# Stage 1's attention shares divided ahead of their transposes, two block sums of V on GpSimd, and a new order

## The chip, the cores and the metric

One core of a Trainium2 chip runs the whole program. The metric is the device time of one execution in microseconds, as the median of the runs; lower is better. TensorE (PE) multiplies, VectorE (DVE), ScalarE (ACT) and GpSimd (POOL) work on tiles, and SyncE (SP) issues nearly all transfers. Each engine takes its instructions strictly in the order in which they stand in its own queue.

## The reference

Attention with a window and with block summaries, and a feed-forward network on its result. Four batches of eight heads, 768 tokens, heads of 64; the model has 512 columns, the network 2048.

```python
k_sum = k.reshape(B, H, nb, block, D).max(axis=3)       # block = 32
v_sum = v.reshape(B, H, nb, block, D).mean(axis=3)
scores_l = scale * q @ k.T, masked to |i - j| < 16
scores_s = scale * q @ k_sum.T + log(block)
a = softmax(concat(scores_l, scores_s))
x = a @ concat(v, v_sum)                  # 3072 tokens x 512
h = x @ w_in; out = (h * sigmoid(h)) @ w_out
```

## The kernel before

A stage is 128 tokens of one batch, 24 in all; a chunk is two stages, 256 tokens. A stage's sixteen half-heads are worked through in two quads of four rows of scores, each 128 x 120: 96 near keys and 24 block summaries. For a quad `scores` makes products on PE, DVE adds the mask and takes the row's extreme (L752), ACT takes exp and sums the row (L756), PE transposes the shares (`turn`, L781), and ACT or DVE copies them out of PSUM into a `tt` tile (L267, L271). `job_c` then multiplies the turned shares with V (L810), which gives the stage's part of x in a PSUM bank, and `job_x` moves it to SBUF. The first four stages (s < `NPL`) work in float32 throughout.

The shares must be divided by the row sums. For the stages in the tuple `EVEN` the function `shares` does that ahead of the transposes: two small DVE instructions make the reciprocals of a quad's sums (L760, L761) and one multiplication over the quad, 128 x 480 (L768 on DVE or GpSimd, or four ACT instructions of 128 x 120, L275), divides. For the first four stages outside that tuple, which before is stage 1 alone, the division waits until x: in `job_x` four small DVE instructions make reciprocals as pairs of float16 parts (L866 to L870), sixteen PE products spread them over the columns (`over`, L877), ACT copies the result to `xr`, and DVE multiplies it onto x (L883).

The sums of V over the blocks of batch 0 are made in `job_mean`: four transfers bring V turned, 128 x 768 each, DVE sums each over blocks of 32 (L631, four instructions) and takes its largest magnitude (L633, four); PE turns the sums back (`turn_sums`, L651) and five copies of 24 x 512 scale them to means, two for each of the stages 0 and 1 and one in `vms`. PE also turns near rows of V for the stages 0 and 1 (L645).

Chunk 0, the stages 0 and 1, opens the feed-forward part. Its x, `xp`, goes in float32 into the first products with the first weights (L1051), which need both halves of `xp` and the first block of weights, unpacked by ACT (L966), GpSimd or DVE or ACT (L957 to L961), and DVE (L968). Everything later on PE is half precision in two parts (L1059, L1068, L1140, L1191, L1262).

The order is not computed at build time: `ORDER` is a string of three characters for each operation, which names the operation and the engine it takes, and `replay` walks it. Before the first products with `xp` the program puts filling matmuls (L387) on PE wherever its own model of time sees PE waiting; they read a constant and their result is not used. After L1051 there are none.

Of the kernel before, what the change touches and what calls it, by code (L numbers as in the profile page):

```python
# [22 lines left out]
BLK = 32  # L23
# [33 lines left out]
EVEN = (0, 2, 3)  # L57
# [203 lines left out]
def local_attn_ffn(ctx: ExitStack, tc: tile.TileContext, q0, qkT, qF, qkD, kF, v, vR, w, out):  # L261
    nc = tc.nc
# [98 lines left out]
    vm_t = vmp_t[:, :, HWIN:]  # L361
# [20 lines left out]
    t_t = ring(NT2, [P, 2 * CH], F32, "t")  # L382
# [4 lines left out]
    plan = Plan(tc, lambda: nc.tensor.matmul(out=bank[0][:, :2 * P], lhsT=unit[:, :P], rhs=unit, start=True, stop=True))  # L387
# [230 lines left out]

    def job_mean(prio):
# [4 lines left out]
        for j in range(4):  # L624
            stg, key = staging(-1)
            nc.vector.memset(stg[:, :HALO], 0.0)
            vr = stg[:, HALO:HALO + S]
# [3 lines left out]
            plan.op({"dve": 869}, lambda e, vr=vr, j=j: nc.vector.tensor_reduce(out=vm_t[:, j, :], in_=vr.rearrange("p (n k) -> p n k", k=BLK), axis=AX.X, op=ALU.add),  # L631
                    r=key, w=[("vm", j)], prio=prio, port=())
# [901 lines left out]
```

## Time and profile before

| | us |
|---|---|
| median of 3 runs | 561.45 |
| the three runs | 560.96, 561.45, 561.95 |
| the profiled execution, its own time | 561.11 |
| its span, first to last instruction | 559.3 |
| PE busy | 552.3 |
| DVE busy | 478.6 |
| ACT busy | 398.3 |
| POOL busy | 191.1 |

Times below are microseconds from the first instruction of the profiled execution. A line number is that of the source of the kernel before; L267, L271, L275, L277, L279, L282 and L285 are lines of small helpers that many operations share, so an instruction is told by its tiles.

### The profile page before, as it was taken

To read this page: it belongs to the slowest core of one execution; us is meant where nothing else is said; L and a number is where in the kernel's file an instruction comes from. 1 tells how busy PE (TensorE), PEld (TensorE's weight loads), DVE (VectorE), ACT (ScalarE), POOL (GpSimd) and SP (SyncE) were. 2 spreads that over 40 slices of the span, in tenths; PEclk is the share of its full clock that TensorE was granted. 3 is DMA by queue.
4 is the path that set the end of the run, shared out by engine and by line. 5 is a ranking of instruction groups with operands and counts; after the bars stand their busy time and mean duration, and the time that the engine had idled before them with its cause. 6 is when DMAs were issued, how large, how long until landed. Compare 5 with 4: busy or idle time off the path is not lost.

```text
span 559.3 us, 15075 instructions
## 1 busy us (share of the span) xinstructions
PE 552.3 (99%) x5821; PEld 392.6 (70%) x5821; DVE 478.6 (86%) x1232; ACT 398.3 (71%) x977; POOL 191.1 (34%) x220
## 2 busy tenths in 40 slices
PE   8999999999999999999999999999999999999997
PEld 6777666676756776666666667666667765688886
DVE  7999999999989899877877777888688769899995
ACT  3999999978886976568775765874776664467441
POOL 1442442342343520322335241331531652224312
PEclk9999999999999999999999999999999999999999
DMA  8899926486735663275353476443375122010002
GB/s 335 353 315 382 406 60 217 99 226 169 168 88 158 187 150 87 95 159 123 116 118 115 154 193 170 128 106 71 129 152 142 50 50 66 1 39 1 2 1 75
DMA packets 64407, 79.09 MB, mean 141 GB/s; under 512 B 46192, under 2 KB 47472, under 8 KB 62288
## 3 DMA queue, kind: packets, MB, share of 16 engines
q1 hardware_dynamic: 64192, 78.01, 48.5%
q8 instruction: 45, 0.74, 0.6%
q14 instruction: 26, 0.21, 0.1%
q10 hardware_dynamic: 144, 0.13, 0.1%
HBM read 59.18 MB, written 6.29 MB: 117 GB/s over the span
## 4 chain that ended last, share of the span: by engine, by line
PE 95%; ACT 1%; DVE 1%; DMA 1%; issue 1%; POOL 0%; SPq 0%; DVEq 0%; POOLq 0%
PE bank L1140 26%; PE bank L1191 22%; PE bank L1068 16%; PE bank L1059 14%; PE bank L1262 7%; PE bank L727 3%; PE bank L828 3%; PE bank L1051 1%; DMA wt<-in_kF_dram 1%; ACT e L756 1%; PE bank L810 0%; PE bank L781 0%; ACT wt L275 0%; PE bank L482 0%; PE bank L554 0%
## 5 line engine op out<-in xcount | busy, mean ns | idle before, releaser
L1140 PE MATMUL bank<-wt 128*128 128x256 f16 x1248 | 152.9, 273 | 0.0
L1140 PEld LDWEIGHTS <-wt 128*128 128x128 f16 x1248 | 121.1, 98 | 30.0
L1068 PE MATMUL bank<-wt,g 128*128 128x512 f16 (+1 forms) x352 | 97.4, 419 | 0.0
L756 ACT ACTIVATE e<-e,mx 128x120 f32<-128x120 f32 x192 | 73.8, 388 | 23.1 <-DVE mx L752 22.7
L1059 PE MATMUL bank<-xh,wt 128*128 128x256 f16 x480 | 86.3, 273 | 0.0
L1059 PEld LDWEIGHTS <-wt 128*128 128x128 f16 x720 | 69.8, 98 | 16.5 <-issue 3.4
L1191 PE MATMUL bank<-wt,g 128*128 128x512 f16 x288 | 69.7, 379 | 0.0
L1059 PE MATMUL bank<-xl,wt 128*128 128x256 f16 x240 | 65.4, 272 | 0.0
L1119 ACT ACTIVATE t<-bank,asc 128x512 f32<-128x512 f32 x48 | 32.4, 686 | 28.2 <-PE bank L1140 28.1
L752 DVE CUSTOM_DVE_ANT_0 e<-bank,masks,qsc 128x120 f32<-128x120 f32 x144 | 42.7, 338 | 7.8 <-PE bank L727 7.3
L1068 PEld LDWEIGHTS <-g 128*128 128x128 f16 x288 | 27.9, 98 | 27.2 <-ACT wt L275 0.2
L1191 PE MATMUL bank<-wt,xl 128*128 128x512 f16 x192 | 45.9, 379 | 0.0
L1191 PEld LDWEIGHTS <-g 128*128 128x128 f16 x288 | 27.9, 98 | 24.6
L1120 DVE SCALAR_TENSOR_TENSOR t<-t,bank 128x512 f32<-128x512 f32 x48 | 32.5, 684 | 12.8 <-ACT t L1119 11.9
L285 POOL TENSOR_TENSOR p<-e,p 128x480 f16<-128x480 f32 x21 | 23.0, 1098 | 42.5 <-ACT p L267 9.6
L756 ACT ACTIVATION_READ_ACCUMULATOR e<-e,mx 128x1 f32 x192 | 36.9, 192 | 0.0
L285 POOL TENSOR_TENSOR g<-t,g 128x512 f16<-128x512 f32 x25 | 29.0, 1160 | 12.0 <-DVE wt L1231 4.4
L1191 PEld LDWEIGHTS <-xl 128*128 128x128 f16 x192 | 18.7, 98 | 17.6
L269 POOL TENSOR_SCALAR g<-t 128x512 f16<-128x512 f32 x19 | 11.8, 620 | 47.6 <-DVE t L1120 18.7
L275 ACT ACTIVATE wt<-bank 128x256 f16<-128x256 f32 (+2 forms) x40 | 16.7, 470 | 14.5 <-PE bank L828 12.2
L282 DVE SCALAR_TENSOR_TENSOR vv<-raw,vsc,vv 120x1024 f16<-120x1024 f32 x19 | 24.3, 1281 | 1.4 <-ACT vv L275 1.1
L1077 ACT ACTIVATE t<-bank,asc 128x512 f32<-128x512 f32 x30 | 20.6, 688 | 6.2 <-PE bank L1059 5.8
(275 smaller groups left out, 1153.5 us busy)
## 6 DMA issues: line engine op xcount, KB each, us to landing
wt<-in_w_dram SPq DMA_DIRECT2D x16, 1024.0 KB
raw<-in_qkD_dram SPq DMA_DIRECT2D x18, 624.0 KB
raw<-in_v_dram SPq DMA_DIRECT2D x20, 512.0 KB
out_dram<-raw SPq DMA_DIRECT2D x20, 256.0 KB
raw<-in_kF_dram SPq DMA_DIRECT2D x12, 384.0 KB
raw<-in_qF_dram SPq DMA_DIRECT2D x9, 512.0 KB
raw<-in_vR_dram SPq DMA_DIRECT2D x12, 384.0 KB
raw<-vms SPq DMA_DIRECT2D x40, 48.0 KB
```

What stands on the lines that cost most here:

```text
L282: nc.vector.scalar_tensor_tensor(out=out, in0=in_, scalar=by, in1=less, op0=ALU.mult, op1=ALU.subtract)
L285: eng[e].tensor_tensor(out=out, in0=in0, in1=in1, op=ALU.subtract)
L752: plan.op({"dve": 195 if b == 0 else 255}, lambda e, k=k, at=at, et=et, mx=mx: nc.vector.tensor_tensor_reduce(out=et, in0=bank[k][:, at:at ...
L756: plan.op({"act": 375}, lambda e, et=et, mx=mx, total=total: nc.scalar.activation(out=et, in_=et, func=AF.Exp, scale=-1.0, bias=mx, accum_ ...
L1059: nc.tensor.matmul(out=h[:, d * CH:(d + 1) * CH], lhsT=wt[f, 0][:, part, d, ct * P:(ct + 1) * P], rhs=x[:, ct, :], start=(ct == 0 and q == ...
L1068: nc.tensor.matmul(out=bank[to][:, :z0 - a0], lhsT=a[:, d * CH + u * P:d * CH + u * P + P], rhs=b[:, d, a0:z0], start=(opens and d == 0 an ...
L1077: plan.op({"act": 586}, lambda e: nc.scalar.activation(out=t, in_=h, func=AF.Tanh, scale=half_z), r=[("bank", k)] + ([] if bare else [("as ...
L1119: plan.op({"act": 586}, lambda e: nc.scalar.activation(out=t, in_=h, func=AF.Tanh, scale=asc_t[c // 3 % 2][:, f:f + 1]), r=[("bank", k), ( ...
L1120: plan.op({"dve": 605}, lambda e: nc.vector.scalar_tensor_tensor(out=t, in0=t, scalar=1.0, in1=h, op0=ALU.add, op1=ALU.mult), r=[("bank", ...
L1140: nc.tensor.matmul(out=to, lhsT=w2[part][:, ct * P:(ct + 1) * P], rhs=xs[j][:, x, ct, :], start=(opens and ct == 0 and q == 0), stop=(ct = ...
L1191: nc.tensor.matmul(out=bank[to], lhsT=a[:, d * CH + v * P:d * CH + v * P + P], rhs=wt[f, 1][:, b][:, d, :], start=(opens and d == 0 and q ...
L1262: nc.tensor.matmul(out=place(m), lhsT=a[pa], rhs=b[pb], start=(opens and not right and q == 0), stop=(closes and q == 2), skip_group_check ...
```

## The change

`EVEN` takes in stage 1, so that its two quads go through `shares` and its x is only copied. `block_sums` lets the plan place a block sum of V on GpSimd, as a tree of five additions over 16, 8, 4, 2 and 1 of the elements of each block, with the second of the two `t` tiles as its scratch. `ORDER` is new. In the new source all lines from L619 on stand 9 or 10 lower.

```diff
-EVEN = (0, 2, 3)
+EVEN = (0, 1, 2, 3)
...
+    def block_sums(e, out, src):
+        if e == "dve":
+            nc.vector.tensor_reduce(out=out, in_=src.rearrange("p (n k) -> p n k", k=BLK), axis=AX.X, op=ALU.add)
+            return
+        part = t_t[1][:, :S // 2].rearrange("p (n k) -> p n k", k=BLK // 2)
+        x, k = src.rearrange("p (n k) -> p n k", k=BLK), BLK // 2
+        while k:
+            nc.gpsimd.tensor_tensor(out=part[:, :, :k] if k > 1 else out.unsqueeze(2), in0=x[:, :, :k], in1=x[:, :, k:2 * k], op=ALU.add)
+            x, k = part, k // 2
...
-            plan.op({"dve": 869}, lambda e, vr=vr, j=j: nc.vector.tensor_reduce(out=vm_t[:, j, :], in_=vr.rearrange("p (n k) -> p n k", k=BLK), axis=AX.X, op=ALU.add),
-                    r=key, w=[("vm", j)], prio=prio, port=())
+            plan.op({"dve": 869, "pool": 2800}, lambda e, vr=vr, j=j: block_sums(e, vm_t[:, j, :], vr), r=key, w=[("vm", j), ("t", 1)], prio=prio, port=("pool",))
...
 ORDER = (
-    "01500v01k00l00800b01f01z02e0040ct01b02t0380ug0111kl0aa00r0bb0b10bh0ah0ar0b700h0ax0an08c0bl0bq0bv04b03m0he08j09d0by0qa08p"
+    "01500v01k00l00b01f01z02e1l200403801b0ct02t0qa0111kl0aa1ks00r0ah0ar0an0b10bb0ax00h0b70bh08c0bl0bq02702a0bw04b03m0he09d0s8"
```

The order differs on every engine up to a point that the kernel before reaches between about 170 and 200 us, and from there each engine's queue is word for word the old one. Over the whole program PE loses the sixteen products of L877 and gains seven filling matmuls (69 to 76), all of them ahead of the first L1051. DVE has four L631 before and two sums of that kind now; it gains seven low-part subtractions of shares (L285, 128x480), four of activations (L285, 128x512), eight additions of weights (L935), two L983 and one L768, and loses three L961. ACT gains eight divisions of 128x120, five L957 and seven casts of 128x512. GpSimd gains the ten additions and loses what DVE and ACT gained.

The three places below are in the start, ahead of the first L1051. First DVE, from the end of stage 1's scores (bank_173 and bank_174 hold its second quad; ss, sh and sum hold row sums; bank_172 the turned block sums). Before:

```order
L752 ISA e,mx<-bank_173,band 128x120
L752 ISA mx 128x1
L633 TENSOR_REDUCE am<-wt 128x1 x2
L866 TENSOR_SCALAR ss_146<-ss_146 128x8
L507 TENSOR_REDUCE am<-am 128x1
L271 COPY wt<-bank_178 96x4x8x16
L867 RECIPROCAL ss_146<-ss_146 128x8
L279 TENSOR_SCALAR wt<-bank_172 24x4x8x16
L869 CAST sh_148<-ss_146 128x8
L870 TENSOR_TENSOR sh_148<-ss_146,sh_148 128x8
```

and now:

```order
L621 TENSOR_REDUCE vm<-wt 128x24
L761 ISA e,mx<-bank_174,band 128x120
L761 ISA mx 128x1
L507 TENSOR_REDUCE am<-am 128x1
L271 COPY wt<-bank_177 96x4x8x16
L769 TENSOR_SCALAR sum_142<-sum_142 128x4
L770 RECIPROCAL sum_142<-sum_142 128x4
L777 TENSOR_TENSOR e<-e,sum_142 128x480
L279 TENSOR_SCALAR wt<-bank_172 24x4x8x16 x2
L271 COPY wt<-bank_173 120x512
```

The last block sum now stands ahead of the last scores of stage 1, and the four small instructions of its late division have made way for the division of the quad and for two copies of means instead of one.

Second ACT, between the copies of the means (bank_172) and the first exp behind them, with both halves of xp (from bank_178 and bank_177, the x of the stages 0 and 1) and the unpacking of the weights (L966, now L975). Before:

```order
L275 ACTIVATE wt<-bank_172 24x4x8x16
L267 COPY wt<-bank_173 120x512
L966 ACTIVATE wt<-wt 128x512
L267 COPY xr_151<-bank_172 128x512
L267 COPY xp<-bank_178 128x4x128
L966 ACTIVATE wt<-wt 128x1024
L966 ACTIVATE wt<-wt 128x512
```

and now:

```order
L275 ACTIVATE wt<-bank_172 24x4x8x16
L975 ACTIVATE wt<-wt 128x512
L275 ACTIVATE wt<-bank_172 24x4x8x16
L267 COPY wt<-bank_175 120x512
L975 ACTIVATE wt<-wt 128x1024
L267 COPY xp<-bank_178 128x4x128
L975 ACTIVATE wt<-wt 128x512
L267 COPY xp<-bank_177 128x4x128
```

ACT now makes both halves of xp, and two unpackings stand between the means and the second half.

Third GpSimd, from the clearing of vm. Before:

```order
L362 MEMSET vm 128x4x96
L768 TENSOR_TENSOR e<-e,sum_140 128x480
L1319 MEMSET p 128x16x8
L959 TENSOR_SCALAR wt<-wt 128x1024
L340 AFFINE_SELECT masks<-masks 64x96
```

and now, from the second block sum on (t_167 is the scratch; five like additions, for another tile of V, and all the masks stand ahead of them):

```order
L626 TENSOR_TENSOR t_167<-wt 128x384
L626 TENSOR_TENSOR t_167<-t_167 128x24x8
L626 TENSOR_TENSOR t_167<-t_167 128x24x4
L626 TENSOR_TENSOR t_167<-t_167 128x24x2
L626 TENSOR_TENSOR vm<-t_167 128x24
L777 TENSOR_TENSOR e<-e,sum_140 128x480
L968 TENSOR_SCALAR wt<-wt 128x512 x2
L968 TENSOR_SCALAR wt<-wt 128x1024 x3
```

The division that GpSimd did first (then for stage 0's second quad) now stands behind the ten additions and is for stage 1's first quad.

## Rows read from the trace of the kernel before

**Rows 1.** The page: span, and busy time of each engine.

```profile
span 559.3 us, 15075 instructions
PE 552.3 (99%) x5821; PEld 392.6 (70%) x5821; DVE 478.6 (86%) x1232; ACT 398.3 (71%) x977; POOL 191.1 (34%) x220
```

**Rows 2.** Waits of PE: what for, us in total, times, longest.

```profile
PE bank L387 <- POOL ident masks.py:199: 1.4, 1, 1.4
...
PE bank L877 <- ACT wt L275: 0.3, 1, 0.3
```

**Rows 3.** Stretches: busy us (instructions) of each engine, granted clock, DMA share, GB/s.

```profile
0.00:26.10 26.10, 22.88 (x380) 17.91 (x380) 21.87 (x93) 16.09 (x49) 7.95 (x23) 1.00 0.88 338
26.10:44.20 18.10, 18.10 (x161) 13.10 (x162) 17.46 (x52) 18.06 (x50) 6.45 (x8) 1.00 1.02 337
44.20:100.00 55.80, 55.80 (x421) 38.10 (x422) 53.24 (x117) 55.15 (x104) 20.50 (x24) 1.00 0.71 254
```

**Rows 4.** Timeline of PE: start, us, line, tiles, count, [idle before].

```profile
11.40 0.62 PE L781 MATMUL bank<-ident,e 128*120 128x128 f32 x4 [0.33 <-DVE e L768]
...
18.27 0.40 PE L727 MATMUL bank<-wt,qk 64*64 64x96 f32 x8
...
19.34 0.26 PE L727 MATMUL bank<-km,qk 64*64 64x24 f32 x8
...
21.85 1.15 PE L810 MATMUL bank<-wt 120*64 120x64 f32 x32
23.26 0.64 PE L877 MATMUL bank<-unit,sh 128*64 128x128 f16 x16 [0.26 <-ACT wt L275]
...
24.95 1.05 PE L387 MATMUL bank<-ident 128*128 128x256 bf16 x8
26.09 5.44 PE L1051 MATMUL bank<-xp,wt 128*128 128x256 f32 x24
```

**Rows 5.** Timeline of DVE in the start.

```profile
10.59 0.66 DVE L768 TENSOR_TENSOR e<-e,sum 128x480 f32<-128x480 f32 x1
...
13.99 0.25 DVE L752 CUSTOM_DVE_ANT_0 e<-bank,band 128x120 f32<-128x120 f32 x1
...
14.78 2.67 DVE L631 TENSOR_REDUCE vm<-wt 128x24 f32<-128x768 f32 x3
...
21.89 0.70 DVE L279 TENSOR_SCALAR wt<-bank 24x512 f32<-24x512 f32 x1
...
22.82 0.17 DVE L870 TENSOR_TENSOR sh<-ss,sh 128x8 f16<-128x8 f32 x1
...
25.14 0.69 DVE L883 TENSOR_TENSOR xp<-bank,xr 128x512 f32<-128x512 f32 x1
```

**Rows 6.** ACT: a group of the page, then its timeline.

```profile
L756 ACT ACTIVATE e<-e,mx 128x120 f32<-128x120 f32 x192 | 73.8, 388 | 23.1 <-DVE mx L752 22.7
...
12.26 0.56 ACT L267 COPY wt<-bank 120x512 f32<-120x512 f32 x1
...
22.62 0.59 ACT L275 ACTIVATE wt<-bank 24x512 f32<-24x512 f32 x1 [0.76 <-DVE wt L279]
...
24.76 0.62 ACT L267 COPY xp<-bank 128x512 f32<-128x512 f32 x1
25.24 1.77 ACT L966 ACTIVATE wt<-wt 128x1024 f32<-128x1024 f32 x2
...
121.87 1.26 ACT L275 ACTIVATE e<-e,sum 128x120 f32<-128x120 f32 x4 [0.52 <-DVE sum L761]
```

**Rows 7.** GpSimd: a group by form (mean ns), then timeline rows, one of DVE.

```profile
L935 POOL TENSOR_TENSOR wt<-wt 128x256 f32<-128x256 f32 x20 | 14.5, 730 | 28.6 <-DVE vv L282 8.6 <-DVE wt L282 5.6 <-DVE g L285 4.4
...
14.23 0.99 POOL L768 TENSOR_TENSOR e<-e,sum 128x480 f32<-128x480 f32 x1 [11.25 <-DVE sum L761]
...
40.06 1.99 POOL L277 TENSOR_SCALAR asc<-ur,vsc 128x1 f32<-128x1 f32 x2
...
40.02 1.23 DVE L968 SCALAR_TENSOR_TENSOR wt<-wt 128x1024 uint32<-128x1024 uint32 x1
```

More of the change, by code (lines that the diff above doesn't have):

```diff
@@ new lines @@
+    "09308j03r09j04g08t0sx02p0by09908p08z0c609n09s03j02m09y0ev04l0fc03w0080fm0410fi0a00fw0f20fs03404q0a80f802z0cx0g204y0g60gb"
+    "0d40gi0490do0de05p05u03e05z0da0640500du05505a05f0dy0dk0v50gj07a0qn05m0e40xd06e06c0e80ug0ed07d0ei06m01u01p06q0r20qh0el0lu"
+    "06v0sl0710c80es0gr0sf07k07p0gt07u07z0qq0cg0so0qw0hn0h10r50t41c70kh0ta0k70hu0kn0jx0i40760jn0td1cc0rb0hj0840kd0io0890vi0ti"
+    "0k30lz1d10jt1ck0rf0ie0ia0kr0kw0ik0l10yw0ri0i01d60wo0cm1co0iu1lj0vc0iy11t0j30tn0cp1cw0us0j80vl0xk0jb0rp0xq0vq1de0l40jj1cr"
@@ new lines @@
+    "0xt0lc0un0h71di0tq0m30xz0tx0vx0uw0vy0le0zl0on0y50u40w50ma0ot0wh0o30n40mg0ox0y61dl0u81410yd0mu0mk0od0yi0ha0p30yo0wk1dq0lm"
+    "0ys0na0oj1dv0o90ru0mq0lq0wc0n01e031d0wv0p70ne1kv0pc0nj1fl0z81eh1ez0ph1lo0no1e80wz0pk0su0s11ec1690nr13c1f40pr0nz1140x41en"
+    "1ri1l90pu0z31l40s41fc1eu17s1200zc15k1rx0q21fg0zy1ep0zs0q60uc1251gd1fr1010xa1gi12914d1fy1lw1061gq14816m1gu1hc1ga16g10b1lz"
+    "1ft0v216p1qy1h01hh0zi14h1h71hp2yd16u13j11h1ht10e1ib13o1g51i010l12e10s14n10x1i61ro11b12l13s1ig1ru1711sr13y2yg1ja1lf110184"
@@ new lines @@
+    "1m214r11k1io12m17z1jf12t1n31351oc1is11q1h21881iy1jn1s315x14u1j515r1r31511jr15d1mj1jx1p61om1qo1721sx1vd18e34h1qj1601ra1k4"
+    "1381661vi1791pc18i1ow1qv18n1m91n91re1oi18q1t31wh1301mt1sc1p218x1os1921tq2yl1i11mp1971pg15g1kh1s919c1wm19h1mz19m1t619r156"
+    "1vq1pl2ys1si1b61j01ps1vu1mf1ba1w020n1so19w1nd1wu1w41jz1tg1tx1ni1u61wy1px1q01x41wc1bh1bq22x1q42371kb1xl17k1x826d1bk1no1xq"
+    "1bu1tn1xg17o1xy25j1w71td17e23r1nu1y223d1yp1nx1y81u137j1am21e1o626j1u91ye1yu1c020u1q921423h1ug2331xb1ul23n21o26p21k34k1z2"
@@ new lines @@
+    "37m1c41yk1uq1uv1v01yf3ry2fx1z625q1v51va21a34p23x2412461o11zc1zg1zo26526921021u21y24c25f27m27s25v24g22322922e24l24p25z277"
+    "3uy1zj1zv1zz2g22ga2h12052ge24u22k22r2092a82d21ac2gk2b92bf1a32dc2d82h62az2gq1a62b51qd20g4192he27d27j3s320k2hi2ho22m2gw2cs"
+    "2af2al2i52ia2ii2gr2hs2i01ax2ci3s827y2im2ap2is24y26s26y2ek2yw2742co2av2j92iy2j42561aq2je3v32bj2bo2fe2822er2f625a2hv41e2ew"
+    "29p28531i2fa2f02py1ag28c2cy2di2dm2x529u2dr2jm2jq2bu2bz2c32c72cc28f28m28r28w2912jv2k02dx2e22xa2xi2xm2iz2q52qa3sd2qk29629b"
@@ L1435 @@
+    "3wu3wz4713w747744a44e46h46n4bd3ep3wc3q744u3ez3ti44k3ju3je4543sl4673wh3x73wp3xb3qc3vj41t3yk3um3jl3xg3xl46d4583yx3vn46x3jp"
+    "3xt47b47g45d47l45i47r3jx45o3z23k447v3k945u47z4013za3qj3ze4613wk3ke3zj3yq3zo45w4063kj3qn4843zw3ko40e3kt3ky3yu3xo40i41x424"
     "40n40s4bs4214bi48843w4bw42949048v4944bm48g3zr42h4994cu48l4c049o49f41042l49l49u48p42r4gk4az4b24a34dn4ds4ai4a94ad40v4e042v"
@@ L1473 @@
+    "9np9jo9nv9uv9t09n09uq9nz9v59t49te9v09pi9vf9lt9va9w79py9wb9vk9po9q49vp9wl9lu9wg9pu9wq9vz9wu9vu9xk9q59x09xo9ho9xa9qx9x49xe"
+    "9r19qa9lz9r69rb9qp9rg9qf9sa9rk9qk9se9rq9s09ru9s4")
 NUDGE = {}
```

66 lines of the change are left out of this document (23 added, 43 removed).

## The prediction, made before the changed kernel was run

> **What bounds the kernel now.** I read the page first, then PE's waits, then the stretches, then the start engine by engine. The page has PE busy for 552.3 of 559.3 us [rows 1]. A busy PE alone proves little here, because the ends of matmuls are modelled; so I looked for what PE waits for. There are six waits in the whole execution, 3.1 us together, the first at the very start and the last ahead of the spreading products of stage 1 [rows 2]. All lie ahead of 26.09 us, where the first products with the weights begin [rows 4]. Behind that point each stretch shows PE busy to the hundredth, at a granted clock of 1.00 [rows 3]. So the execution has two parts: a start of 26.09 us, in which PE follows the attention of the stages 0 and 1 and fills its gaps with matmuls that nobody reads, and some 533 us in which PE is fed without a break. From the first L1051 on, the change removes no matmul and adds none. The time therefore moves by what the first L1051 moves, plus any gap that opens later; the later part has none to give back.
>
> Two other engines are close behind. Between 44.2 and 100 us DVE is busy for 53.24 and ACT for 55.15 of 55.80 us [rows 3].
>
> **The change, part by part.** *What goes.* Sixteen spreading products on PE, 0.64 us [rows 4]; four small DVE instructions like the last of them, 0.17 each, 0.7 together, and the multiplication onto x, 0.69 [rows 5]; one ACT copy like that of xp, 0.62 [rows 6]; two block sums on DVE, 0.89 each by the three that took 2.67, 1.8 together [rows 5]. PE's 0.64 is worth nothing by itself: PE does not set the start, and the new order puts seven fillers more, 0.13 each by the eight that took 1.05 [rows 4], 0.9 us, into gaps ahead of the first L1051. Their cover is PE's wait there; without it they would cost their 0.9 and eat the 0.64.
>
> *What comes.* Four small DVE instructions for the two quads' reciprocals, 0.7 by the same price; one quad divided on DVE, 0.66 [rows 5], which replaces that of stage 0's first quad; one on GpSimd, 0.99 [rows 7]; the two quads of stage 0 divided on ACT instead, 1.26 each [rows 6]; a second copy of means on DVE, 0.70 [rows 5]; an xp copy on ACT, 0.62 [rows 6].
>
> *The ten additions on GpSimd* have no row. Their 24 blocks of 16, 8, 4, 2 and 1 elements make 384, 192, 96, 48 and 24, 744 in all. The nearest row is an addition of 128x256, 730 ns [rows 7]. All-in by the element that is 2.1 us for a block sum; the upper end takes all five at the price of the 128x480 row, 0.99 [rows 7], 4.95 us. I take 2.7, near the lower end, since three of the five are far smaller than any row. A gain below nothing is excluded: GpSimd did not do them before.
>
> *The start, added up again.* I follow the changed queues with these prices.
>
> 1. Stage 0's first quad has its reciprocals at 10.6, where DVE divided it, until 11.25 [rows 5]. ACT needs until 11.9. PE's transposes, at 11.40 before [rows 4], come 0.6 later.
> 2. ACT's four exps of the second quad, 0.39 each [rows 6], stand behind the division and end at 13.4, and the copy of the turned first quad behind them at 13.95; before it ended at 12.82 [rows 6]. Stage 1's scores go into that bank, so they wait for it: 1.1 us later than before.
> 3. One half of a stage's scores takes 0.65, half of the 1.33 from 18.27 to 19.60 [rows 4]: 14.7. DVE reads four rows of scores in 0.79, from 13.99 to 14.78 before [rows 5], and now until 15.5.
> 4. Here the two sums that DVE lost pay. Behind those reads it has one maximum and one sum, 0.9 each, two small ones, three reads, the second sum and the last read: 1.8 + 0.35 + 0.6 + 0.9 + 0.2 = 3.9, so 19.4. The last exp and its sum take 0.6: 20.0. Then the small ones 0.4, the division 0.66, the two copies of means 0.65 each: 22.4. Before, the last of its small ones ended at 22.99 [rows 5]. The 1.1 us lost in step 2 have been won back.
> 5. ACT waits for the second copy of means, as it did before [rows 6], and then has six instructions up to the second half of xp: a copy of means 0.5, a copy of shares 0.5, an unpacking of 1024 and a copy, an unpacking of 512 and the last copy. By [rows 6] the two unpackings are 1.77 and the copies 0.5 from start to start, the last 0.62: 0.5 + 0.5 + 1.77 + 0.5 + 0.6 = 3.9, less 0.15 that the overlap of starts takes off: 26.1.
> 6. PE meanwhile: stage 0's product with V when the means are copied, 21.9 to 23.0; stage 1's, when its last turned quad is copied, 23.5 to 24.6; and stage 2's scores, 1.33: 25.9 [rows 4]. So ACT's 26.1 decides, by 0.2.
>
> The first L1051 begins at 26.1, where it began at 26.09. The difference is nothing, with some 0.6 us either way, because six steps were priced to a tenth.
>
> *What the first part hands on.* Behind the first L1051 come sixteen of them, the first L1068, the transposes of stage 2 and scores of stage 3. The new order has done less of stage 2 by then. Its two quads are divided on DVE by my sum at 31.5 and 34.1, and PE reaches their transposes at 35, so 0.9 us cover the second.
>
> *GpSimd against DVE.* At 40.06 two GpSimd instructions on one element each took 1.99 us while DVE's L968, which reads two tiles, ran for 1.23 from 40.02 [rows 7]. So the two engines can hold each other up, and the additions read two tiles. Between the first and the last of them the new order has no such DVE instruction, only maxima, reads of scores and the reciprocals of four sums; I price the meeting at nothing. The Trainium skill, SBUF — State Buffer, section "SBUF: two separate sides", says that the pair of ports that DVE and GpSimd share is held for a whole instruction and that the other engine stands still meanwhile. By that rule a small DVE instruction that needs the pair could stand behind one addition, and the start would be up to one addition, 1.0 us, later; the row agrees that such stops happen, and shows them only on GpSimd's side.
>
> **The sum.** The profiled execution took 561.11, of which 559.3 is the span and 1.8 lies around it. Its start stays, so 561.1 on its own scale. The median of the runs is 561.45, 0.34 above it; on that scale, which the result will have, 561.4.
>
> **The rivals.** *Slower: GpSimd holds stage 1 up.* Its division of stage 1's first quad stands behind the ten additions. The first five start at 10.6 and the second five after 13.8, where the order has them wait for DVE's reciprocals; the division can start at 17.9. At 2.7 a sum they end at 16.5, so 1.4 us are free. At the upper end, 4.95, they end at 20.5, the division at 21.5 instead of 18.9, and the turning of the sums, which stands behind the transposes of that quad, moves from 20.0 to 22.2; part of it runs into time that ACT waits anyway, and the first L1051 comes 1.7 later: 563.1. It decides from 3.5 us a sum on. For it speaks that five dependent instructions each have a start to pay; against it the 730 ns for 256 elements. 0.12.
>
> *Slower: PE is no longer fed.* The new order takes work off GpSimd and gives it to DVE and ACT, which have 2.6 and 0.65 us idle between 44.2 and 100 [rows 3]. Seven and four subtractions at about the 0.66 of a 128x480 instruction [rows 5] and eight additions at half of it are 9.9 us more on DVE, and five unpackings at about 1.1 [rows 6] are 5.5 more on ACT, over the whole reordered part. If a microsecond or two of it falls where PE waits, it is 562.6 to 563.5. For it speaks how full both are; against it that most of the moved subtractions come later, when both have more room. 0.10.
>
> *Faster: the start shrinks.* The DVE work of the start loses 1.8 + 0.7 + 0.69 and gains 0.7 + 0.70 + 0.6 for a copy of shares, 1.2 less in all. If ACT's divisions in steps 1 and 2 run beside other waits and don't delay the scores, the first L1051 comes up to that much earlier, 24.9, and the time is 560.2. Against it: ACT's last six instructions do not get shorter. 0.12.
>
> *The change does nothing for the path:* the removed products are replaced by fillers. That is my forecast itself, 0.66.
>
> **How the numbers follow.** The likeliest case gives 561.4 and by its own doubt 560.8 to 562.0. The range reaches to the faster rival, 560.2, and to the slower ones, 563.1, with about half of each inside. 0.2%, 1.1 us, is about what a measurement of this kernel tells from no change. Faster by more than that: 0.12. Within it: 0.66. Slower by more: 0.12 + 0.10 = 0.22.
>
> **What would show it.** In the changed profile the first L1051 should begin between 25.5 and 26.7 and PE should show no wait behind it. The waits list should have no L877, and ACT's second xp copy should end right ahead of the L1051. The five additions of a sum should take 2.1 to 3.5 us, and GpSimd's division should start at about 17.9 on DVE's reciprocals. If the first L1051 begins at 27 or later with stage 1's transposes waiting for GpSimd, the first rival holds; if PE shows gaps between 44 and 120 us on DVE or ACT, the second; if the start ends by 25.0, the third.

## The result, and the profile after

The changed kernel takes 565.19 us (median of six runs, 564.81 to 566.69), the kernel before 561.49 in the same series (560.96 to 561.95): 1.0072 times as long, 95% interval 1.0057 to 1.0088. The forecast was 561.4 with a range up to 563.1, so it was wrong, and on the wrong side of "no change". The profiled execution took 565.39 us, with a span of 563.6.

A line number is now that of the changed source: what was L1051, L1059, L1068 and L1140 is L1060, L1068, L1077 and L1149, and L991 and L968 are L1000 and L977. The page's span and busy times, to be read beside [rows 1]:

```profile
span 563.6 us, 15063 instructions
PE 554.3 (98%) x5812; PEld 392.9 (70%) x5812; DVE 482.0 (86%) x1251; ACT 404.5 (72%) x991; POOL 173.0 (31%) x201
```

GpSimd has lost 18 us of work, DVE and ACT have gained 3.4 and 6.2. PE's waits, which were six, all ahead of the first product with the weights [rows 2] (what for, us in total, times, longest):

```profile
PE bank L387 <- POOL ident masks.py:199: 1.4, 1, 1.4
PE bank L998 <- POOL wm L1000: 0.7, 1, 0.7
PE bank L736 <- ACT wt L267: 0.6, 2, 0.3
PE bank L1149 <- DVE t L1129: 0.5, 1, 0.5
PE bank L819 <- DVE sc L517: 0.5, 1, 0.5
PE bank L1060 <- ACT xp L267: 0.4, 1, 0.4
PE bank L1077 <- DVE g L285: 0.4, 1, 0.4
...
PE bank L736 <- DVE qk L595: 0.2, 1, 0.2
```

L998, L1149, L1077 and the L736 that waits for qk lie behind the first L1060. PE is no longer fed without a break, and that is where most of the time of this profile went. PE's timeline gives the places (start, us, tiles, count, idle before it):

```profile
26.80 5.45 PE L1060 MATMUL bank<-xp,wt 128*128 128x256 f32 x24 [0.44 <-ACT xp L267]
...
40.58 0.38 PE L998 MATMUL bank<-wm,spread 128*128 128x2 f32 x2 [0.71 <-POOL wm L1000]
...
45.74 0.27 PE L1068 MATMUL bank<-xh,wt 128*128 128x256 f16 x1
...
192.27 1.04 PE L1077 MATMUL bank<-wt,g 128*128 128x512 f16 x4 [0.40 <-DVE g L285]
...
242.75 1.47 PE L1149 MATMUL bank<-wt 128*128 128x256 f16 x12 [0.47 <-DVE t L1129]
```

The idle times understate the loss, because the records of neighbouring matmuls overlap: from the start of one matmul to the start of the next, the gap at 192.27 costs 0.56 us and that at 242.75 costs 0.63. Three smaller gaps, ahead of the matmuls at 175.6, 196.4 and 204.2, cost 0.31, 0.42 and 0.25; only the one at 196.4 (L736, waiting for qk) is in the list of waits. That is 1.54 us in four gaps between 171 and 208, and 0.63 in a fifth.

Four stretches add up to the span, by the first start of each of three lines in PE's timeline: up to the first L1060, from there to the first L1068, from there to the first L1149, and the rest. From the first L1060 on, each stretch holds the same number of matmuls in both kernels.

| us | before | after | more |
|---|---|---|---|
| to the first L1060 | 26.09 | 26.80 | 0.71 |
| to the first L1068 | 18.07 | 18.93 | 0.86 |
| to the first L1149 | 177.46 | 179.44 | 1.98 |
| to the end | 337.71 | 338.43 | 0.72 |

The stretch from 137 to 208 us shows what is different late (columns as in [rows 3]); first the kernel before, then the changed one:

```profile
137.00:208.00 71.00, 71.00 (x792) 49.35 (x791) 63.65 (x156) 56.95 (x148) 27.46 (x32) 1.00 0.60 156
```

```profile
137.00:208.00 71.00, 70.16 (x823) 47.92 (x821) 67.00 (x171) 60.79 (x162) 3.30 (x4) 1.00 0.63 165
```

GpSimd does next to nothing for 70 us, DVE and ACT do 3 to 4 us more. But DVE does not only work there, it also stands. Its waits between 95 and 215 us, and the places in its timeline:

```profile
DVE km L458 <- DMA raw<-in_kF_dram: 2.4, 2, 1.2
...
DVE vm L536 <- DMA raw<-in_vR_dram: 0.7, 1, 0.7
```

```profile
171.76 0.95 DVE L458 TENSOR_REDUCE km<-raw 128x24 f32<-128x768 f32 x1 [1.18 <-DMA raw<-in_kF_dram]
...
190.66 0.95 DVE L458 TENSOR_REDUCE km<-raw 128x24 f32<-128x768 f32 x1 [1.21 <-DMA raw<-in_kF_dram]
191.53 0.68 DVE L285 TENSOR_TENSOR g<-t,g 128x512 f16<-128x512 f32 x1
```

3.1 us in all; the kernel before has no such wait in that stretch. The last two rows are the link to PE: the low half of g (L285) stands behind the maximum of kF in DVE's queue, the maximum waits for its load, and PE's L1077 at 192.27 waits for the low half. The fifth gap has the same form: at 241.15 DVE has waited 1.32 us for a load of V, L1129 stands behind that load's reader, and PE waits for L1129. But there the queues are the old ones again; e13 below shows that gap with the old order too, so that it is no mark of the new one.

### The profile page after: what moved, and what is told of

It reads as the page before. It is cut to its first block, busy times and chain, and to the rows that moved or that the text cites. A ratio compares the mean times of both kernels' runs of the same rounds, so it can differ in the third digit from the quotient of the medians.

```text
span 563.6 us, 15063 instructions
## 1 busy us (share of the span) xinstructions
PE 554.3 (98%) x5812; PEld 392.9 (70%) x5812; DVE 482.0 (86%) x1251; ACT 404.5 (72%) x991; POOL 173.0 (31%) x201
## 4 chain that ended last, share of the span: by engine, by line
PE 84%; DMA 5%; DVE 5%; ACT 4%; issue 1%; POOL 1%; SPq 0%; DVEq 0%; ACTq 0%
PE bank L1149 25%; PE bank L1200 21%; PE bank L1077 12%; PE bank L1068 10%; PE bank L1271 7%; PE bank L736 3%; PE bank L837 3%; DMA raw<-in_kF_dram 1%; PE bank L1060 1%; ACT e L765 1%; DMA out_dram<-raw 1%; DMA wt<-in_kF_dram 1%; DMA raw<-in_vR_dram 1%; DMA raw<-in_qF_dram 1%; DVE e L761 1%
## 5 line engine op out<-in xcount | busy, mean ns | idle before, releaser
L1149 PE MATMUL bank<-wt 128*128 128x256 f16 x1248 | 153.1, 273 | 0.5 <-DVE t L1129 0.5
L1149 PEld LDWEIGHTS <-wt 128*128 128x128 f16 x1248 | 121.1, 98 | 30.7 <-issue 0.6
L1077 PE MATMUL bank<-wt,g 128*128 128x512 f16 (+1 forms) x352 | 97.8, 419 | 0.6 <-DVE g L285 0.4
L1068 PE MATMUL bank<-xh,wt 128*128 128x256 f16 x480 | 86.0, 273 | 0.0
L1068 PEld LDWEIGHTS <-wt 128*128 128x128 f16 x720 | 69.9, 98 | 16.8 <-issue 3.8
L1068 PE MATMUL bank<-xl,wt 128*128 128x256 f16 x240 | 65.4, 273 | 0.0
L1128 ACT ACTIVATE t<-bank,asc 128x512 f32<-128x512 f32 x48 | 32.2, 684 | 26.5 <-PE bank L1149 26.2
L1077 PEld LDWEIGHTS <-g 128*128 128x128 f16 x288 | 27.6, 98 | 29.5 <-DVE g L285 2.1
L1129 DVE SCALAR_TENSOR_TENSOR t<-t,bank 128x512 f32<-128x512 f32 x48 | 32.5, 683 | 12.3 <-ACT t L1128 11.7
L944 POOL TENSOR_TENSOR wt<-wt 128x256 f32<-128x256 f32 x12 | 8.8, 730 | 87.1 <-DVE g L285 70.3
L285 POOL TENSOR_TENSOR g<-t,g 128x512 f16<-128x512 f32 x21 | 24.4, 1160 | 13.4 <-DVE wt L1240 4.4
L285 POOL TENSOR_TENSOR p<-e,p 128x480 f16<-128x480 f32 x14 | 15.4, 1099 | 38.9 <-ACT p L267 20.6
L275 ACT ACTIVATE e<-e,sum 128x120 f32<-128x120 f32 x80 | 24.9, 382 | 1.6 <-DVE sum L770 1.4
```

The source lines that it names most:

```text
L275: nc.scalar.activation(out=out, in_=in_, func=AF.Copy, scale=by)
L285: eng[e].tensor_tensor(out=out, in0=in0, in1=in1, op=ALU.subtract)
L1068: nc.tensor.matmul(out=h[:, d * CH:(d + 1) * CH], lhsT=wt[f, 0][:, part, d, ct * P:(ct + 1) * P], rhs=x[:, ct, :], start=(ct == 0 and q == ...
L1077: nc.tensor.matmul(out=bank[to][:, :z0 - a0], lhsT=a[:, d * CH + u * P:d * CH + u * P + P], rhs=b[:, d, a0:z0], start=(opens and d == 0 an ...
L1128: plan.op({"act": 586}, lambda e: nc.scalar.activation(out=t, in_=h, func=AF.Tanh, scale=asc_t[c // 3 % 2][:, f:f + 1]), r=[("bank", k), ( ...
L1129: plan.op({"dve": 605}, lambda e: nc.vector.scalar_tensor_tensor(out=t, in0=t, scalar=1.0, in1=h, op0=ALU.add, op1=ALU.mult), r=[("bank", ...
```

## The experiments

Each order below is one of the two known ones, or one with few operations moved; the arithmetic is the whole kernel's in all of them. Diffs of queues show instructions of one engine. The table has the stretches of every profile, as above, and DVE's waits for loads between 95 and 215 us (the sum of the rows that name a transfer); the time is a median with its ratio to the kernel before, in runs on the same chip.

| kernel | first L1060 | to L1068 | to L1149 | to the end | DVE waits for loads | time | ratio (95%) |
|---|---|---|---|---|---|---|---|
| before | 26.09 | 18.07 | 177.46 | 337.71 | 0 | 561.49 | |
| after | 26.80 | 18.93 | 179.44 | 338.43 | 3.1 | 565.19 | 1.0072 (1.0057 to 1.0088) |
| e1 | 26.53 | 18.92 | 177.77 | 338.33 | 0 | 563.49 | 1.0031 (1.0020 to 1.0042) |
| e2 | 26.66 | 18.93 | 177.80 | 337.95 | 0 | 563.14 | 1.0022 (1.0014 to 1.0031) |
| e3 | 26.97 | 18.98 | 179.47 | 337.71 | 3.4 | 566.89 | 1.0087 (1.0069 to 1.0106) |
| e4 | 26.80 | 18.16 | 179.33 | 337.63 | 3.0 | 564.95 | 1.0056 (1.0043 to 1.0068) |
| e5 | 26.81 | 18.96 | 180.49 | 337.63 | 4.4 | 566.20 | 1.0085 (1.0059 to 1.0111) |
| e6 | 26.88 | 18.08 | 178.16 | 337.82 | 0.2 | 562.75 | 1.0017 (1.0009 to 1.0026) |
| e7 | 26.98 | 18.08 | 178.06 | 337.63 | 0 | 562.53 | 1.0014 (1.0004 to 1.0023) |
| e8 | 27.65 | 18.96 | 182.39 | 338.40 | 6.3 | 569.02 | 1.0124 (1.0111 to 1.0137) |
| e9 | 26.77 | 18.92 | 178.61 | 339.50 | 2.2 | 565.33 | 1.0060 (1.0047 to 1.0072) |
| e10 | 27.30 | 18.97 | 177.87 | 338.26 | 1.3 | 564.23 | 1.0043 (1.0031 to 1.0056) |
| e11 | 27.02 | 18.16 | 178.38 | 337.76 | 1.7 | 563.60 | 1.0034 (1.0021 to 1.0046) |
| e12 | 26.70 | 18.49 | 177.46 | 338.45 | 0 | 562.17 | 1.0007 (0.9998 to 1.0016) |
| e13 | 26.73 | 18.47 | 177.96 | 338.91 | 1.1 | 562.24 | 1.0000 (0.9991 to 1.0009) |
| e14 | 26.62 | 18.95 | 179.35 | 337.66 | 2.6 | 563.95 | 1.0035 (1.0022 to 1.0047) |
| e15 | 26.53 | 18.16 | 178.21 | 338.10 | 1.9 | 563.56 | 1.0026 (1.0016 to 1.0036) |

e6, e12 and e13 are the kernel before with an edit, so their lines are L1051, L1059 and L1140, and the buffers added in e9 to e12, e14 and e15 move them on by 3 or 5. A profile is one execution, the time a median of several; single stretches of one order differ by some tenths.

**e1: the changed kernel up to 95 us, then the old order.** The end of `ORDER` is replaced: behind the operations that the changed order's plan starts before 95 us, the rest stands in the old sequence and on the old engines. GpSimd's queue there, a piece:

```diff
-L944 TENSOR_TENSOR wt<-wt 128x256
 L285 TENSOR_TENSOR g_169<-t_166,g_169 128x512
-L944 TENSOR_TENSOR wt<-wt 128x256
...
+L285 TENSOR_TENSOR p<-e,p 128x4x120
+L285 TENSOR_TENSOR g_168<-t_166,g_168 128x512
+L944 TENSOR_TENSOR wt<-wt 128x256
```

> The changed kernel with its own order for the first 95 us of the plan, and behind that the order and the choice of engines of the kernel before. Theory 'starved late': from 137 to 208 us GpSimd has nothing to do, VectorE does its subtractions, and TensorE waits there and up to 242 us for VectorE (0.31 + 0.56 + 0.42 + 0.25 + 0.63 = 2.2 us in five gaps). Then these gaps go, the lead of 1.6 us that is lost by 45.7 us stays, and the time is 562.9 us (562.5 to 563.3). Rival 'backlog': the edits have put VectorE behind by 95 us, and any order waits then: 564.5 to 565.3 us, with TensorE waiting for VectorE behind 100 us as in the changed kernel.

Measured 563.49; the interval leaves 0.20 to 0.42% of the 0.72. The third stretch falls from 179.44 to 177.77 us, DVE waits for no load, and the stretch that PE could not fill is full again:

```profile
137.00:208.00 71.00, 71.00 (x832) 49.19 (x831) 63.91 (x155) 56.96 (x151) 27.48 (x31) 1.00 0.63 161
```

Some 2 us of the loss, more than half, belong to the order and the choice of engines behind 95 us and not to the edits. The time is 0.6 us above the likeliest value expected and 0.2 above its range; the backlog that the rival foresaw is not there.

**e2: the changed kernel up to 40 us, then the old order.** The same edit with an earlier cut.

> The changed kernel with its own order for the first 40 us of the plan only, and behind that the order and engines of the kernel before. Theory 'start and order apart': the new start costs 0.7 to 1.6 us and all the rest is the order behind it, so 562.3 to 563.3 us, likeliest 562.8. Rival 'the edits cost': the GpSimd sums and the added divisions displace work that has to be done later whatever the order: 564.5 us or more.

563.14, inside the first theory's range. Between e1 and e2 lies what the new order does from 40 to 95 us: 0.35 us by the medians, with intervals that overlap, so it may be nothing.

**e3: the table load first.** ScalarE's queue:

```diff
+L275 ACT_TABLE_LOAD
+L275 ACTIVATE unit_149<-ident 128x128
 L577 DMA qk_123<-in_q_dram 128x256
-L765 ACT_TABLE_LOAD
...
-L275 ACTIVATE unit_149<-ident 128x128
```

> The changed kernel with the small ScalarE op on the unit matrix first on ScalarE again, so that the table load lies ahead of the first q load on ScalarE's queue, as in the kernel before. Theory 'early load': that q load, issued at 0.73 us instead of 1.35, delays the first kF by 0.54 us, and the chain behind it by 0.4: the first reduction of kF is at 4.1 again, the first score eviction's exp at 8.5, the first product with the weights (L1060) at 26.4 instead of 26.8, time 564.8 us. Rival: the kF load is later for another reason, or the 0.4 us are lost again in the start's later waits: first L1060 at 26.7 or later, time 565.2 us.

The first theory falls. The first reduction of kF is at 4.10 us again, but the third, which the scores wait for, is at 7.91 (7.71 after, 7.33 before), and the first L1060 at 26.97; the time, 566.89, is not lower than the changed kernel's. The table also shows how little a single start says: with the changed start it lies anywhere from 26.53 to 27.30 us, 26.80 on average over eleven profiles (without e3 and e8); with the old one at 26.09, 26.70, 26.73 and 26.88. So of the 0.71 us between the two profiled executions most may be luck of the old one: on average it is 0.2, by only four old starts, two of them (e12, e13) from the slowest execution of their kernel, and a 0.2 of so few can't be told from no change.

**e4: one clamp on VectorE.**

```diff
 L1002 SCALAR_TENSOR_TENSOR ur<-bank_177,flip 128x2
+L1000 TENSOR_SCALAR wm<-wm 128x1
 L977 SCALAR_TENSOR_TENSOR wt<-wt 128x1024
```

> The changed kernel with one of its tiny clamps of a weight maximum (L1000, 128x1) on VectorE instead of GpSimd, ahead of the 1.29 us pass of L977 beside which GpSimd took 1.07 us for it. Theory 'lock': TensorE's wait of 0.71 us at 39.9 us falls under 0.2, the first L1068 comes at 45.1 instead of 45.7 and the time falls to 564.6 us. Rival: the clamp was late for another reason, or the next wait (the second clamp behind ScalarE's maximum) takes its place: the first L1068 stays within 0.2 us of 45.7, time 565.2 us.

In the changed kernel the two clamps (128x1) lie beside DVE's pass over two tiles; GpSimd's timeline, then DVE's:

```profile
38.68 0.69 POOL L277 TENSOR_SCALAR xh<-xp,vsc 128x512 f16<-128x512 f32 x1 [1.36 <-DVE wt L977]
39.45 1.25 POOL L1000 TENSOR_SCALAR wm<-wm 128x1 f32<-128x1 f32 x2
```

```profile
39.16 1.29 DVE L977 SCALAR_TENSOR_TENSOR wt<-wt 128x1024 uint32<-128x1024 uint32 x1
```

The first, 1.07 us of the 1.25, ends at 40.53, just behind the pass (40.45), the second at 40.70. With one of them on DVE, in e4:

```profile
39.22 0.15 DVE L1000 TENSOR_SCALAR wm<-wm 128x1 f32<-128x1 f32 x1
39.28 1.23 DVE L977 SCALAR_TENSOR_TENSOR wt<-wt 128x1024 uint32<-128x1024 uint32 x1
...
39.81 0.38 PE L998 MATMUL bank<-wm,spread 128*128 128x2 f32 x2
39.98 0.61 POOL L1000 TENSOR_SCALAR wm<-wm 128x1 f32<-128x1 f32 x1 [0.54 <-ACT wt L990]
```

PE's wait is gone and the first L1068 comes at 44.97, 0.77 earlier: the mechanism is shown. The time is lower by 0.24 only (0.16% by the ratios, with overlapping intervals), so how much of the 0.77 reaches the end is not shown; part of it may be waited away later.

**e5: eleven operations back on GpSimd.** Between 143 and 193 us, a piece of GpSimd's queue:

```diff
 L944 TENSOR_TENSOR wt<-wt 128x256 x3
...
+L269 TENSOR_SCALAR g_168<-t_166 128x512
+L944 TENSOR_TENSOR wt<-wt 128x256 x3
+L285 TENSOR_TENSOR p<-e,p 128x4x120
...
 L285 TENSOR_TENSOR p<-e,p 128x4x120
```

> The changed kernel in its own order, with 11 operations between 143 and 193 us (low halves of g and p, casts, sums of weights) moved from VectorE to GpSimd, where the kernel before has them. VectorE gets 4.2 us lighter by the plan's costs, GpSimd is no longer idle from 137 to 208 us. Theory 'starved late': TensorE's waits for VectorE between 130 and 245 us go, from the first L1068 to the first L1149 it takes 178.0 us or less instead of 179.4, time 563.6 us (563.0 to 564.2). Rival 'the order itself': what makes TensorE wait is the order of VectorE's work, or GpSimd's slower operations become what TensorE waits for: 179 us or more for that stretch, time 565 us.

It missed: 566.2 us, which can't be told from the changed kernel's time, and 180.49 us for the stretch, as the rival had it. DVE's work from 137 to 208 us is down to the old 63.7 us, and PE loses more there than in the changed kernel:

```profile
137.00:208.00 71.00, 69.52 (x818) 47.52 (x817) 63.71 (x162) 60.48 (x163) 12.76 (x15) 1.00 0.67 166
```

```profile
PE bank L1077 <- DVE g L285: 1.3, 1, 1.3
```

DVE's waits for loads have grown to 4.4 us. The low halves of g that PE waits for have stayed on DVE, behind the same maxima. So a lighter DVE alone does not feed PE in this order, and the theory as it was put falls; the waits for loads took its place.

**e6: the mirror image on the kernel before.** 23 operations of GpSimd between 95 and 208 us on DVE and ACT, its own order otherwise; a piece of GpSimd's queue:

```diff
 L269 TENSOR_SCALAR p<-e 128x4x120
 L285 TENSOR_TENSOR p<-e,p 128x4x120
 L935 TENSOR_TENSOR wt<-wt 128x256
-L285 TENSOR_TENSOR p<-e,p 128x4x120
 L285 TENSOR_TENSOR g_168<-t_166,g_168 128x512
-L935 TENSOR_TENSOR wt<-wt 128x256
-L277 TENSOR_SCALAR wt<-wt,uk 128x1024
```

> The mirror image on the kernel before: its own code, start and order, with 23 operations between 95 and 208 us moved from GpSimd to VectorE (7.3 us by the plan's costs) or ScalarE (2.1 us), as the changed kernel has them. Theory 'starved late': TensorE waits for VectorE behind 100 us, the stretch from the first L1059 to the first L1140 grows from 177.5 us to 178.5 or more, time 563.0 us (562.3 to 564.5). Rival: VectorE's 65 us of work in 71 has room for it and the time stays at 561.8.

562.75, within the first theory's range but with a stretch of 178.16, under the 178.5 expected. DVE works as long as in the changed kernel and waits for loads for 0.2 us; PE has one new wait in the stretch:

```profile
137.00:208.00 71.00, 70.47 (x826) 48.73 (x823) 67.45 (x168) 58.43 (x155) 16.60 (x17) 1.00 0.65 161
```

```profile
PE bank L1068 <- DVE raw L1110: 0.5, 1, 0.5
```

So the moved work does cost something by itself: 0.17% (0.09 to 0.26), some 0.9 us. In the stretch it is 0.7 us in this one profile, a third of what the changed kernel loses there; the profiles of the old order with DVE at 64 us run from 177.46 to 178.06.

**e7: the edits of e2 and e4 together.**

> The changed kernel with its own order for the first 40 us, the order of the kernel before behind it, and the one clamp (L1000) on VectorE. If the two losses add, TensorE's wait of 0.7 us at 40 us goes and is not made up for later, since nothing behind is starved: 562.4 us (562.0 to 562.8), first L1068 at 44.9. If the clamp's gain is eaten by a later wait, as its time alone leaves open: 563.1 us.

562.53: the two gains add within the intervals, and 0.04 to 0.23% of the 0.72 are left. These are the changed kernel's edits with the old order behind 40 us, and it is still a little slower than the kernel before.

**e8: both block sums back on VectorE.**

```diff
 L761 ISA mx 128x1
+L621 TENSOR_REDUCE vm<-wt 128x24
 L761 ISA e,mx<-bank_173,band 128x120
...
 L642 TENSOR_REDUCE am<-wt 128x1
+L621 TENSOR_REDUCE vm<-wt 128x24
```

> The changed kernel with the two block sums of GpSimd back on VectorE (0.94 us each instead of 2.83), ahead of the maxima that stand there now. Theory 'the sums on GpSimd help the start': VectorE's queue up to 16 us gets 1.9 us longer, of which its gaps hide about 1.0, so the first L1060 comes at 27.3 to 27.8 us and the time is 565.9 us. Rival 'GpSimd's sums cost': the first L1060 comes at 26.8 or earlier, time 565.2 us or less.

The first L1060 is at 27.65, as the first theory had it, but the time is 569.02. A start that is 0.85 us later became 3.8 us; the other 2.95 lie in the third stretch, with twice the waits for loads:

```profile
DVE km L458 <- DMA raw<-in_kF_dram: 3.9, 2, 2.4
DVE vm L536 <- DMA raw<-in_vR_dram: 2.4, 2, 2.2
```

GpSimd's sums are a gain to this start. And in this order that delay grew on its way.

**e9 and e10: buffers of their own for late loads.** The three `raw` buffers serve loads and stores in turn. e9 gives the four kF loads of the third batch two buffers; e10 also one vR load of the second.

```diff
+    kraw = ring(2, [P, S], F32, "kraw")
...
+            if b == 2:
+                stg, key = kraw[hp in (0, 3)], [("kraw", hp in (0, 3))]
...
+            if b == 1 and j == 1:
+                stg, key = kraw[0], [("kraw", False)]
```

> The changed kernel in its own order, with two buffers of their own for the four kF loads of the third batch (164 to 190 us), which otherwise share the three raw buffers with the output's stores and the other loads; VectorE's work is the same. Theory 'late loads': VectorE stands for 1.2 us at 171 and 1.2 us at 190 waiting for these loads, and the low halves of g that stand behind in its queue make TensorE wait; with the loads issued earlier both waits go, from the first L1068 to the first L1149 it takes 178.3 us or less instead of 179.4, time 563.9 us (563.3 to 564.5). Rival 'VectorE is too full': the waits for the loads go but TensorE waits for VectorE all the same, 179 us or more, time 565 us.

> As the run before, and the second batch's vR load that VectorE waits for at 122 us has one of the two buffers too. Theory 'late loads': the 0.7 us wait at 122 us goes too and with it TensorE's wait at 131 us (L514, 0.4 to 0.8 us in some profiles): 563.6 us (563.0 to 564.2), and the runs lie within 1.2 us of each other, where the changed kernel's lie within 1.9. Rival: the same time as the run before or 565 us.

DVE's waits for loads fall from 3.1 to 2.2 and 1.3 us, and the third stretch from 179.44 to 178.61 and 177.87. e9's time stays, though. In its profile PE has lost 0.9 us to a late transfer of turned shares at 269.6, behind the stretch (L840 is e9's line for L837); whether its other executions lose the same is not known:

```profile
269.61 0.76 PE L840 MATMUL bank<-tt,vv 120*64 120x64 f16 x36 [0.86 <-DMA tt<-p]
```

e10 is at 564.23, a little above its range, with its runs within 1.1 us; its interval and the changed kernel's just miss each other. Nothing but buffers has changed here, and none of the four gaps between 171 and 208 us is left, so the waits for loads do cost PE time. The load for 171 us still comes 0.76 us late in e10, and costs nothing there.

**e11: e10 and the clamp of e4.**

> As the run before, and the one clamp (L1000) on VectorE. If late loads and the lock are the two losses behind the start, only the start is left: 562.9 us (562.3 to 563.5). If the order has more losses than these: 563.5 us or more.

563.60: the second reading, by 0.1 us. With the waits for loads down to 1.7 us and the lock gone, the order by its median still costs more than e7; the intervals overlap a little.

**e12 and e13: the kernel before with its loads changed.** e12 has the buffers of e9. e13 delays two kF loads, on SyncE's queue alone:

```diff
+L592 DMA raw_121<-in_qkD_dram 128x1248
 L457 DMA raw_120<-in_kF_dram 128x768
 L457 DMA raw_122<-in_kF_dram 128x768
-L592 DMA raw_121<-in_qkD_dram 128x1248
```

> The kernel before with the same two buffers for the same four kF loads. Its profile shows no wait of TensorE behind 26 us, so by the theory 'late loads' nothing is there to be gained: 561.9 us (561.5 to 562.3). If the buffers help whatever the order, it falls by 0.5 us or more.

> The kernel before with one change: on the queue of SyncE the load of q and k for the next stage (L592) goes ahead of the two kF loads that stood ahead of it at 185 and 186 us of the plan. Every other engine's order is the same. Theory 'late loads': VectorE, which waits for no load there before, then waits 1 to 2.5 us for them at about 190 us, the low half of g behind it in its queue is late, TensorE waits, and from the first L1059 to the first L1140 it takes 178.2 us or more instead of 177.5; time 562.7 us (562.3 to 563.6). Rival 'only VectorE's load counts': VectorE has 7 us to spare between 137 and 208 us, catches up, and the time stays at 561.9 us (561.5 to 562.3).

e12 changes nothing that can be measured. e13 neither, against the theory: its time is what the rival had. DVE does wait, but the low half of g that PE needs stands ahead of the maxima there, and PE does not wait for it.

```profile
190.10 0.69 DVE L285 TENSOR_TENSOR g<-t,g 128x512 f16<-128x512 f32 x1
191.86 1.87 DVE L458 TENSOR_REDUCE km<-raw 128x24 f32<-128x768 f32 x2 [1.08 <-DMA raw<-in_kF_dram]
...
239.25 0.95 DVE L536 TENSOR_REDUCE vm<-raw 128x24 f32<-128x768 f32 x1 [1.44 <-DMA raw<-in_vR_dram]
```

```profile
PE bank L1140 <- DVE t L1120: 0.6, 1, 0.6
```

That a late load costs by what stands behind its reader in the queue of the engine that waits fits this: in the changed order it is the low half of g. e13 does not part it from the rival, that DVE has room to catch up. The last two lines are from later in the same profile, that of the slowest of its eleven executions: there a late load of V has L1120 behind its reader, and PE does wait for it, in the old order. So the old order is not safe from such gaps either; the profile of the kernel before just has none.

**e14 and e15: buffers and GpSimd's work together, and the clamp.** e14 is e10 with the edit of e5, e15 adds that of e4.

> The changed kernel in its own order with both cures at once: own buffers for the four kF loads and the one vR load, and the 11 operations between 143 and 193 us back on GpSimd. Own buffers alone left 0.4 to 1.1 us of the 2.0, the 11 operations alone (with later loads) gave nothing. Theory 'late loads on a full VectorE': with both gone TensorE waits for VectorE no longer between 95 and 215 us, from the first L1068 to the first L1149 it takes 177.8 us or less, and the time is 563.5 us (563.0 to 564.0). Rival 'GpSimd's slower operations are waited for': 178.3 us or more, 564.2 us or more.

> As the run before, with the one clamp (L1000) on VectorE. If start, lock, late loads and a full VectorE are all there is, what is left is the start alone: 562.6 us (562.0 to 563.1), first L1068 at 45.1. If more is left, 563.2 or above.

e14's time is in the range, but its profile, of the slowest of its five executions, is not: DVE has 63.9 us of work and still 2.6 us of waits for loads, and PE waits 1.1 us for g. e15, 563.56, lies where its time was expected if more is left than start, lock, late loads and a full DVE; its interval overlaps with e7's, though.

Over all profiles the third stretch goes with DVE's waits for loads and not with DVE's work: with none or 0.2 us it takes 177.5 to 178.2 us, with 1.1 to 2.2 us 177.9 to 178.6, with 2.6 to 3.4 us 179.3 to 179.5, with 4.4 us 180.5, with 6.3 us 182.4. Each of these is a single profile.

## Why the prediction was wrong

**The step that failed** is the first: "The time therefore moves by what the first L1051 moves, plus any gap that opens later; the later part has none to give back." The sum then put the second term, the gaps that open later, at nothing ("Its start stays, so 561.1"). Behind the first L1060 the profile measured 3.56 us for it: 0.86, 1.98 and 0.72 in the three stretches, of the 4.27 that the span grew. I looked there only for what could be gained and took PE's unbroken stretch over for the new order, as if it were a property of the work. It hangs on the order: nearly the same instructions, in another sequence and in part on other engines, left gaps. e1 shows it by putting the old sequence and engines back behind 95 us, which recovers some 2 us with all edits in place.

**The rival that held** was "PE is no longer fed", at 0.10, with the right part of the program but the smaller part of the mechanism and too small a price (562.6 to 563.5). I counted microseconds of work moved onto DVE and ACT and looked at 44 to 120 us. The gaps lie from 171 to 242 us. e6 shows that moved work has a price, some 0.9 us (562.75), and e5 that it is not the main one: with DVE as light as before in the changed order, PE waited longer. What the prediction did not look at is SyncE's queue and how much earlier than its reader each load lands. The changed kernel is best set beside e1, which has the same start and the old order there. SyncE issues the loads of kF for DVE's two late maxima as follows, first in the changed kernel, then in e1:

```profile
167.22 0.94 SPq L457 DMA_DIRECT2D raw<-in_kF_dram  x1
...
187.46 0.86 SPq L457 DMA_DIRECT2D raw<-in_kF_dram  x2
```

```profile
161.09 0.34 SPq L457 DMA_DIRECT2D raw<-in_kF_dram  x1
...
186.41 2.32 SPq L457 DMA_DIRECT2D raw<-in_kF_dram  x2
```

In e1 DVE comes to read them at 167.19 and 191.26, 6.1 and 4.9 us after the issue, and waits for neither. In the changed kernel it is ready at 170.58 and 189.45, only 3.4 and 2.0 us after; the loads have landed 4.5 and 3.2 us after their issue, and DVE waits 1.2 us for each. So the lead of these loads has shrunk from both sides: they are issued later, and the new order of DVE reads the second one sooner. The waits of SyncE's queue between 95 and 215 us in the changed kernel:

```profile
SPq L804 <- DVE p L285: 9.5, 4, 5.3
...
SPq L457 <- DMA out_dram<-raw: 3.7, 1, 3.7
```

The kF load of 190 us waits 3.7 us (2.0 before) until a store has left its buffer, and transposes (L804) wait for DVE's low halves of p, 9.5 us here against 5.2 before, with loads behind them in the queue. That a late DVE thereby makes its own loads later would explain why 0.85 us at the start became 3.8 in e8; it is argued from these rows and was not tested by itself, and the rows of e8 agree only in part: the wait for the store grows there to 4.4, that for p falls to 7.8.

**The start** was nearly right. The forecast put the first L1051 at 26.1 against 26.09; measured were 26.80, 0.1 outside the 25.5 to 26.7 that it gave as the sign, and on average 26.80 against 26.60. The sizes held: a block sum on GpSimd takes 2.83 us from 11.07 (2.7 forecast, 2.1 to 3.5 as the sign), its division starts at 18.32 (17.9), and ACT's six instructions from the second copy of means take 3.82 (3.9).

```profile
11.07 1.04 POOL L626 TENSOR_TENSOR t<-wt 128x384 f32<-128x384 f32 x1 [2.39 <-DVE sum L770]
12.19 1.40 POOL L626 TENSOR_TENSOR t<-t 128x192 f32<-128x192 f32 x3
13.67 0.23 POOL L626 TENSOR_TENSOR vm<-t 128x24 f32<-128x24 f32 x1
...
18.32 0.99 POOL L777 TENSOR_TENSOR e<-e,sum 128x480 f32<-128x480 f32 x1 [1.16 <-ACT wt L267]
```

Of the 0.7 us, 0.4 were there from step 1: the third load of kF came later (DVE read it at 7.71, before at 7.33), ACT could begin its division at 11.03, and the same 0.4 stand in step 4, whose small instructions started at 20.40 instead of 20.0. The other 0.3 came in the steps 4 and 5: the second copy of means ends at 22.90 for 22.4, the last copy of xp at 26.75 for 26.1. That copy does end right ahead of the first L1060, L877 is gone, PE stands idle for 0.44 us ahead of the first L1060, so that the seven fillers cost nothing, and the 0.9 us of cover in stage 2 held: no transpose waits there. The rival of a held-up stage 1 did not come; e8 shows the opposite, that the sums on GpSimd are worth having.

**The lock between GpSimd and DVE** was priced at nothing. For the additions that was right: DVE's maxima beside them took 0.92 and 0.95 us, and one not beside them 0.95. But the new order also put a clamp on which PE waits beside a pass over two tiles; [rows 7] showed this very stop, 1.99 us for two tiny instructions, and I searched for it only around the additions. It cost PE a wait of 0.71 us, which e4 took away. The Trainium skill, SBUF — State Buffer, section "SBUF: two separate sides", says that of a DVE instruction with two inputs in SBUF and a GpSimd instruction that reads SBUF, whichever starts first keeps the shared ports for its whole instruction; the trace agrees here, since the pass began at 39.16, the first clamp at 39.45, and the clamp ended 0.08 us behind the pass.

**The sum** by the runs: of 0.72%, the order behind 95 us takes about 0.41 (e1), the stretch from 40 to 95 us 0.09 and the clamp 0.08 (e2, e7, each within the intervals' overlap), and 0.14, 0.8 us, stay with the start and what e7 did not undo; of these the starts on average show 0.2. Within the order behind 95 us late loads are shown to cost, by e10's time and by the gaps that are gone from its profile; e6 puts a price on the moved work. What remains open is where the rest of those 0.8 us lies, whether the 0.12% between e15 and e7 is real, since their intervals overlap, and what in the order first makes the loads late.

## What to carry to other kernels

A bottleneck engine that is fed without a break has its margin in the queues that feed it: before a reordering is priced, look for how long each load lands ahead of its reader, and what stands behind that reader in its queue. Counting the microseconds of work that move between the feeding engines told less here; more depended on which instruction must wait for which transfer or shared port, and whether the bottleneck waits behind it. To tell an edit from the order that came with it, run the new start with the old rest: one cut parted them here. And a difference of some tenths between two single profiles should be set beside how far profiles of one kernel lie apart.

## What the runs showed of the hardware

A GpSimd clamp on 128x1 took 0.21 us behind the end of a DVE instruction of 1.29 that reads two tiles, and the one ahead of it, beside that instruction, 1.07 (1.25 for both from 39.45), while additions of two tiles on GpSimd did not lengthen DVE's maxima over one tile. GpSimd's additions in float32 took 1034 ns for 384 elements, 592 for 192, 386 for 96, 268 for 48 and 226 for 24, by the groups of the changed kernel by form.
